# A convolution and an ELU network in one kernel: two start-up convs one step earlier, their writes ahead of the reads

## The chip, the cores and the metric

The kernel runs on one core of one Trainium2 chip. The metric is the device time of one execution in microseconds (us). A core has a tensor engine (PE in the profile; PEld is its weight load), VectorE (DVE), ScalarE (ACT), GpSimd (POOL) and SyncE (SP). Each engine works through its own list of instructions in order; engines wait for each other through semaphores. Transfers (DMA) are issued by SP (queue q1 in the profile) or by GpSimd (queue q0), and run on 16 shared DMA engines.

## What is computed

```python
# x: (8, 4096, 192), weight: (8 heads, 7 taps), w_in: (192, 2048), w_out: (2048, 192)
w = softmax(weight, axis=-1)                       # seven taps per head
x_pad = concatenate([zeros(B, 6, D), x], axis=1)   # causal
idx = arange(S)[:, None] + arange(7)[None, :]
x_unf = x_pad[:, idx, :].reshape(B, S, 7, 8, 24)
a = einsum('hk,bskhg->bshg', w, x_unf).reshape(B * S, 192)
h = a @ w_in
g = where(h > 0, h, exp(minimum(h, 0)) - 1)        # ELU
out = g @ w_out                                    # (32768, 192), float32
```

A causal convolution with seven taps per head, then a network of two layers with an ELU between, for 32768 tokens.

## The kernel before

**Super steps and steps.** The tokens are worked through in 32 super steps `s` of 1024, each in two halves `g` of 512. A super step has 16 steps, one for each 128 columns of the hidden layer; step `n` in this text counts through all of them, so that steps 0 to 15 belong to super step 0, and step 16 is the first of super step 1. One step is: PE multiplies `att` (the convolved tokens) with `w_in` in six matmuls into one of three slots of the PSUM tensor `H` (L706), ScalarE takes the exponential of both halves into `E` (L499), GpSimd limits it (L410), VectorE forms the ELU as `gT` (L561). A slot of `H` is free for step n once VectorE is through with the step that had it, three takers before. Matmuls of the second layer (L741, from `gT` and `w_out` into `ops`) for the super step before are put in the gaps between the steps, by the table `GAPS`.

**Where the convolved tokens come from.** Super step 0 makes its own with small matmuls at the start (L616 to L648). For every later super step there are two convs, one per half, numbered `m = 2*s + g - 2`: conv 0 and conv 1 are halves 0 and 1 of super step 1, conv 2 is half 0 of super step 2. A conv is 40 small matmuls on PE (L679), from a window of `x` (`xg`, loaded by GpSimd at L362 in two parts per super step) and the taps matrix `Tr`. ScalarE copies its result to `csb` (L479), and then it goes over DRAM to change its layout: SP writes `csb` into the bounce buffer in DRAM (`conv_slots`, L773, 256 KB), waits for that to have landed, and reads it back into `att` in three transfers of 64 KB (`read_att`, L334). The first step of super step 1 waits for all six reads of its two halves at L701.

**What sets the order.** The list `order` (L87 to L148) is the schedule that PE, ScalarE and SP all follow: for each step its "h" item, then the convs and second-layer pieces put there. For super step 0 the dictionary `EARLY_CONV` (L37) says after which step a conv comes: conv 0 after step 4, conv 1 after step 7, conv 2 after step 10. Convs 0 to 2 use the PSUM tensor `ops`, which is free at that time; a conv there waits for the copies of the one before (L671). ScalarE copies the first half of such a conv at its place in the order and the second half after the next step's exponentials (L488 to L503); the semaphore `s_ce` counts the second copies. In the first 13 steps PE also does pairs of warm-up matmuls on zeros ahead of a step (L694 to L696), except ahead of the two steps that follow a conv; these write into `ops` and so wait for the copies of the convs so far. Step 10 further waits for a second copy of `w_in`'s last columns (`s_wc`, L700).

**SP's loop** (L768 to L796). At a conv SP waits for its second copy (`s_ce`), issues the write, and then, for conv 0 and for every half 1, calls `read_att` at once, which waits for the write's landing (L327). For half 0 of super steps 2 and later the reads are issued at the second step of the super step before, when `att`'s other buffer is free (L782 to L784). Before the loop SP issues the tap loads and, once the last columns of `w_in` have come, the second copy of these (L766). GpSimd issues its loads at the very start in the order `w_in`, `x`, `w_out` (768 KB), the last part of `x` (L392 to L402).

Of the kernel before, what the change touches and what calls it, by code (L numbers as in the profile page):

```python
# [33 lines left out]
WARM = (9, 1)  # L34

CONV_AT = ((2, 1, 1), (10, 2, 0))
EARLY_CONV = {4: (1, 0), 7: (1, 1), 10: (2, 0)}  # L37
FREE_CONV = 3
QUAD = 4
XTW = 136  # L40
# [11 lines left out]
def bass_lightweight_conv__then__act_elu_kernel(  # L52
# [36 lines left out]
    def conv_at(s, g):  # L89
        m = 2 * s + g - 2  # L90
        if m >= FREE_CONV:
            slot_of_conv[m] = take_slot(("c", m))
        order.append(("c", m))
# [38 lines left out]
    for n in range(NP):  # L132
        s, i = divmod(n, NQ)
# [3 lines left out]
        if len(gaps) == 2:  # L137
            order.append(("o", gaps.pop(0)))
        if n in EARLY_CONV:
            conv_at(*EARLY_CONV[n])  # L140
        if s:
# [44 lines left out]
    with ExitStack() as stack:  # L186
# [111 lines left out]
        def load_first(eng, k):  # L298
            eng.dma_start(
                xf[:, k, :, :].rearrange("p i d -> p (i d)"),  # L300
                x_flat[GS * k : GS * (k + 1), :].rearrange("(p i) d -> p (i d)", i=QUAD),
            ).then_inc(s_xl[k], 16)

        def conv_read(W, m):
            W(s_ce, m + 1)

        def out_group(eng, t, half, g, kb=None):
            b = (2 * t + half) % 2
            row = SUP * t + GS * g + 2 * P * half
            if kb is not None:  # L310
                eng.dma_start(
                    out[row + P * kb : row + P * (kb + 1), :], osb[:, b, g, kb, :]
                ).then_inc(s_out[b], 16)
                return
            dst = out[row : row + 2 * P, :].rearrange("(k p) d -> p k d", p=P)
            if t == 0:
                dst = bass.AP(
                    tensor=out.tensor,
                    offset=(GS * half + 1 - g) * D,
                    ap=[[QUAD * D, P], [2 * D, 2], [1, D]],  # L320
                )
            eng.dma_start(dst, osb[:, b, g, :, :]).then_inc(s_out[b], 16)

        def read_att(eng, W, s, g):

            m = 2 * s + g - 2
            W(s_dw[m % 4], 16 * (m // 4 + 1))  # L327
            for j in range(3):
                src = bass.AP(
                    tensor=bounce.tensor,  # L330
                    offset=(2 * P * (s % 2) + j) * SUP + GS * g,
                    ap=[[SLOT * SUP, HEADS], [3 * SUP, 8], [1, GS]],
                )
                eng.dma_start(  # L334
                    att[HP * g : HP * (g + 1), s % 2, j, :], src
                ).then_inc(s_att[s % 2], 16)
# [240 lines left out]
        def _tensor(pe):  # L577
# [16 lines left out]
            def warm_pair(count):  # L594
                for _ in range(count):
                    for r in range(2):
                        pe.matmul(  # L597
                            ops[:, r, :],
                            zw[HP * r : HP * (r + 1), 0:P],
                            zw[HP * r : HP * (r + 1), :],  # L600
                            start=True,
                            stop=True,
                            tile_position=(HP * r, 0),
                        )
# [56 lines left out]
            for x_, item in enumerate(order):  # L661
# [26 lines left out]
                elif item[0] == "h":  # L688
                    n = item[1]
                    s, q = divmod(n, NQ)  # L690
                    if n == 0:
                        W(s_ha, 2)
                        W(s_hd, 2)
                    elif n < NQ + LAG and not any(n - 2 <= e < n for e in EARLY_CONV):  # L694
                        conv_read(W, sum(e < n for e in EARLY_CONV) - 1)
                        warm_pair(WARM[1])  # L696
# [55 lines left out]
        @block.sync  # L752
        def _sync(sy):
            W = Waits(sy)
            sy.dma_start(wh[:], weight[:, :]).then_inc(s_wd, 16)
            load_first(sy, 1)
            W(s_wp, 1)
            sy.dma_start(taps[:, :], zt[:, :]).then_inc(s_band, 16)
            W(s_band, 16)
            sy.dma_start(  # L760
                Tr[:, :, :],
                bass.AP(tensor=taps.tensor, offset=0, ap=[[1, P], [ZW, HEADS], [1, CW]]),
            ).then_inc(s_band, 16)
            c0, c1 = WCOLS[3]
            W(s_w[3], 16)
            sy.dma_start(w_in[HP:P, :, c0:c1], w_in[0:HP, :, c0:c1]).then_inc(s_wc, 16)  # L766

            for item in order:  # L768
                if item[0] == "c":
                    m = item[1]  # L770
                    s, g = divmod(m + 2, 2)
                    conv_read(W, m)
                    sy.dma_start(  # L773
                        bounce[s % 2, :, :, GS * g : GS * (g + 1)].rearrange("b p t -> p b t"),
                        csb[:, m % 4, :, :],
                    ).then_inc(s_dw[m % 4], 16)
                    if m == 0 or g == 1:

                        read_att(sy, W, s, g)
                elif item[0] == "h":  # L780
                    s, i = divmod(item[1], NQ)
                    if i == 1 and s >= 1 and s + 1 < NS:  # L782
                        W(s_h, NQ * s)
                        read_att(sy, W, s + 1, 0)  # L784
                elif item[0] == "o":
                    for key in item[2]:
                        t, half, kb = key
                        W(s_oev, place[key] + 1)
                        if (t, half) != (last, 1):
                            for g in range(2):  # L790
                                out_group(sy, t, half, g)
                        elif kb == 0:
                            for g in range(2):
                                out_group(sy, t, half, g, 0)
                        else:
                            out_group(sy, t, half, 0, 1)  # L796
            for b in range(2):
                sy.wait_ge(s_out[b], 32 * NS + 32 * b)
# [28 lines left out]
```

## Time and profile before

| | us |
|---|---|
| median of 5 runs | 752.3 |
| the five runs | 752.3, 750.1, 752.6, 749.66, 752.91 |
| the profiled execution, its time | 752.89 |
| the profiled execution, its span | 751.1 |
| matmuls of the first layer, L706 (3072) | 408.5 busy |
| matmuls of the second layer, L741 (8064) | 417.9 busy |
| exponentials, L499 (1024) | 546.2 busy |
| ELU on VectorE, L561 (1024) | 633.2 busy |
| granted TensorE clock, mean | 0.997 of full |

Times in the profile are in microseconds from the start of the span. A row of groups or of the timeline names the line, the engine, the operation and its tiles; matmuls overlap each other, so the sum of their busy times can be more than PE's. A row of waits says which engine at which line waited for whom: in total, how many times, the longest. The chain of waits is followed back from the last instruction: each piece is the work or the transfer that the next one waited for. In the table of busy time by stretch the last columns are the granted clock of TensorE (1.00 is full), the share of the DMA engines and what they moved in GB/s. The DMA queues are given with packets, megabytes and the time that their packets took as a share of 16 engines' span.

### The profile page before, as it was taken

Reading aid. Unit: us, or ns where it says so; the run is one execution under the profiler, and the core shown is the slowest. Engines: PE = TensorE matmul, PEld = TensorE weight load, DVE = VectorE, ACT = ScalarE, POOL = GpSimd, SP = SyncE. Lnnn points to the kernel's source line nnn. Section 1 sums busy time; section 2 is a strip of 40 time slices with the busy share of each in tenths; the row PEclk is TensorE's granted clock in tenths of the full one; section 3 lists DMA queues with packets and bytes.
Section 4 is the critical chain, followed back from the end, with each engine's and each line's share of the span. In section 5 each row is a group of like instructions: output and inputs, shape, how many; then the busy total and the mean of one; then the engine's idle time right before and its main releaser. Section 6 shows DMA issues by size and latency. Waiting matters only on the chain.

```text
span 751.1 us, 32212 instructions
## 1 busy us (share of the span) xinstructions
PE 737.5 (98%) x13850; PEld 517.9 (69%) x13850; DVE 638.2 (85%) x1041; ACT 646.9 (86%) x1165; POOL 661.3 (88%) x1107
## 2 busy tenths in 40 slices
PE   8699999999999999999999999999999999999998
PEld 4367777776777776776777776777776777777666
DVE  5779889889888898898898898898898898898894
ACT  6788888888888988888988888888888888888884
POOL 8789899899899899899898899898899898998883
PEclk9999999999999999999999999999999999999999
DMA  9544434535435535434435345445344344344112
GB/s 176 119 86 102 93 97 103 108 80 108 86 94 112 106 73 118 86 90 112 98 86 117 80 95 108 92 96 114 77 102 107 87 102 102 88 103 105 60 44 65
DMA packets 107039, 72.79 MB, mean 97 GB/s; under 512 B 44553, under 2 KB 106641, under 8 KB 106897
## 3 DMA queue, kind: packets, MB, share of 16 engines
q1 hardware_dynamic: 66384, 54.47, 23.9%
q0 software_dynamic: 40224, 15.78, 19.5%
q8 instruction: 108, 1.77, 1.0%
q10 hardware_dynamic: 288, 0.49, 0.2%
q14 instruction: 35, 0.28, 0.1%
HBM read 44.78 MB, written 41.42 MB: 115 GB/s over the span
## 4 chain that ended last, share of the span: by engine, by line
PE 96%; DMA 2%; ACT 1%; DVE 0%; SPq 0%; issue 0%; POOL 0%
PE ops L741 45%; PE H L706 45%; PE H L679 5%; DMA conv_slots<-csb 1%; PE H L741 1%; DMA xf<-in_x_dram 0%; SPq L334 0%; DMA att<-conv_slots 0%; DVE gT L561 0%; ACT E L499 0%; PE H L648 0%; PE ops L648 0%; ACT csb L479 0%; POOL E L410 0%; ACT xT L438 0%
## 5 line engine op out<-in xcount | busy, mean ns | idle before, releaser
L561 DVE SCALAR_TENSOR_TENSOR gT<-E,H 128x512 f16<-128x512 f32 x1024 | 633.2, 682 | 97.6 <-POOL E L410 91.3
L410 POOL TENSOR_SCALAR E<-E 128x512 f32<-128x512 f32 x1024 | 604.5, 614 | 77.4 <-ACT E L499 72.5
L499 ACT ACTIVATE E<-H 128x512 f32<-128x512 f32 x1024 | 546.2, 605 | 88.8 <-PE H L706 80.2
L741 PEld LDWEIGHTS ops<-w_out,gT 64*128 64x128 f16 x8064 | 346.2, 94 | 107.0 <-ACT osb L470 10.9
L741 PE MATMUL ops<-w_out,gT 64*128 64x192 f16 x8064 | 417.9, 243 | 0.3
L706 PE MATMUL H<-att,w_in 64*128 64x512 bf16 x3072 | 408.5, 377 | 6.3 <-DMA att<-conv_slots 3.6
L706 PEld LDWEIGHTS H<-att,w_in 64*128 64x128 bf16 x3072 | 133.8, 94 | 104.0 <-issue 5.3
L479 ACT ACTIVATE csb<-H 128x1024 bf16<-128x1024 f32 x59 | 60.4, 1024 | 0.0
L470 ACT ACTIVATE osb<-ops 128x768 f32<-128x768 f32 x63 | 51.5, 817 | 6.2 <-PE ops L741 6.2
L362 POOL DMA_DIRECT2D xg<-in_x_dram x62 | 52.3, 843 | 0.4 <-issue 0.4
L679 PE MATMUL H<-Tr,xg 128*24 128x122 bf16 (+1 forms) x2360 | 38.6, 209 | 0.0
L679 PEld LDWEIGHTS H<-Tr,xg 128*24 128x24 bf16 x2360 | 29.5, 92 | 9.3 <-issue 9.3
L741 PE MATMUL H<-w_out,gT 64*128 64x192 f16 x128 | 5.9, 243 | 0.0
L572 DVE COPY osb<-H 128x192 f32<-128x192 f32 x1 | 0.4, 358 | 6.3 <-PE H L741 6.3
L741 PEld LDWEIGHTS H<-w_out,gT 64*128 64x128 f16 x128 | 5.3, 94 | 0.0
L592 PE MATMUL ops<-zw 128*128 128x512 bf16 x9 | 4.0, 628 | 1.2 <-DVE zw L511 1.2
L367 POOL DMA_DIRECT2D w_in<-in_moe_w_in_dram x7 | 4.6, 658 | 0.3 <-DMA wh<-in_weight_dram 0.3
L597 PE MATMUL ops<-zw 64*128 64x512 bf16 x12 | 2.3, 379 | 1.6 <-ACT csb L479 1.6
L479 ACT ACTIVATE csb<-ops 128x512 bf16<-128x512 f32 x6 | 3.7, 622 | 0.0
L592 PEld LDWEIGHTS ops<-zw 128*128 128x128 bf16 x9 | 1.2, 139 | 3.2 <-issue 2.0
L597 PEld LDWEIGHTS ops<-zw 64*128 64x128 bf16 x12 | 0.6, 93 | 3.0 <-ACT csb L479 2.6
L679 PEld LDWEIGHTS ops<-Tr,xg 128*24 128x24 bf16 x120 | 1.5, 92 | 1.3 <-issue 1.3
(47 smaller groups left out, 25.9 us busy)
## 6 DMA issues: line engine op xcount, KB each, us to landing
out_dram<-osb SPq DMA_DIRECT2D x126, 192.0 KB, 2.7
conv_slots<-csb SPq DMA_DIRECT2D x62, 256.0 KB, 2.5
att<-conv_slots SPq DMA_DIRECT2D x186, 64.0 KB
xg<-in_x_dram POOLq DMA_DIRECT2D x31, 240.0 KB, 5.2
xg<-in_x_dram POOLq DMA_DIRECT2D x31, 192.0 KB, 4.5
w_out<-in_moe_w_out_dram POOLq DMA_DIRECT2D x1, 768.0 KB, 15.2
w_in<-in_moe_w_in_dram POOLq DMA_DIRECT2D x2, 240.0 KB, 8.0
xf<-in_x_dram ACTq DMA_DIRECT2D x1, 384.0 KB, 3.2
```

Of the source, the lines that this page charges most:

```text
L362: g.dma_start(xg[:, b, w0:w1, :], src).then_inc(s_x[b][part - 1], 16)
L367: g.dma_start(w_in[HP * r : HP * (r + 1), :, c0:c1], moe_w_in.rearrange("(p j) f -> p j f", j=3)[:, :, c0:c1],).then_inc(s_w[k], 16)
L410: g.tensor_scalar(out=E[:, n % NE, u, :], in0=E[:, n % NE, u, :], scalar1=1.0, scalar2=0.0, op0=ALU.min, op1=ALU.max,).then_inc(s_clp)
L470: a.activation(osb[:, b, :, :, :].rearrange("p g k d -> p g (k d)"), ops[:, :, 0 : 2 * D], ACT.Copy,).then_inc(s_oev)
L479: return a.activation(csb[:, m % 4, b0:b1, :], conv_bank(m)[:, b0:b1, :], ACT.Copy)
L499: a.activation(E[:, n % NE, u, :], H[:, k, GS * u : GS * (u + 1)], ACT.Exp).then_inc(s_exp)
L561: v.scalar_tensor_tensor(out=gT[:, s % NG3, q, u, :], in0=E[:, n % NE, u, :], scalar=1.0, in1=H[:, slot_of_pair[n] % 3, GS * u : GS * (u + ...
L592: pe.matmul(ops[:, 0, :], zw[:, 0:P], zw[:], start=True, stop=True)
L597: pe.matmul(ops[:, r, :], zw[HP * r : HP * (r + 1), 0:P], zw[HP * r : HP * (r + 1), :], start=True, stop=True, tile_position=(HP * r, 0),)
L679: ins = pe.matmul(to[SLOT * q : SLOT * q + CPH, hb, o : o + nc_], xg[:, s % NXB, w, CPH * h : CPH * (h + 1)], Tr[:, h, CW - c0 - nc_ : CW ...
L706: ins = pe.matmul(H[:, k % 3, GS * r : GS * (r + 1)], w_in[HP * r : HP * (r + 1), j, FC * q : FC * (q + 1)], att[HP * r : HP * (r + 1), s ...
L741: ins = pe.matmul(acc[:, g, d0 : d0 + D], gT[HP * rt : HP * (rt + 1), t % NG3, q, g, t0 : t0 + P], w_out[HP * rt : HP * (rt + 1), q, :], s ...
```

## The change

Conv 0 moves from after step 4 to after step 3, and conv 1 from after step 7 to after step 6; conv 2 stays. The pairs of warm-up matmuls follow the convs: before there is one ahead of each of steps 1, 2, 3, 4, 7 and 10, after the change ahead of 1, 2, 3, 6, 9 and 10. On SP, conv 0's write is no longer followed by its reads. At conv 1 SP issues the write of conv 1, then the three reads of conv 0's half, then the three of conv 1's half. Each group of reads still waits for the landing of its own write. All later convs are written and read as before.

```diff
 CONV_AT = ((2, 1, 1), (10, 2, 0))
-EARLY_CONV = {4: (1, 0), 7: (1, 1), 10: (2, 0)}
+EARLY_CONV = {3: (1, 0), 6: (1, 1), 10: (2, 0)}
...
                         csb[:, m % 4, :, :],
                     ).then_inc(s_dw[m % 4], 16)
-                    if m == 0 or g == 1:
-
+                    if m == 1:
+                        read_att(sy, W, s, 0)
+                    if g == 1:
                         read_att(sy, W, s, g)
```

## The prediction

> **What bounds the kernel now.** I read the page's busy shares first, then the waits, then the chain that ended last. The first line below is the page's, the two under it are from the waits of the whole run:
>
> ```profile
> PE 737.5 (98%) x13850; PEld 517.9 (69%) x13850; DVE 638.2 (85%) x1041; ACT 646.9 (86%) x1165; POOL 661.3 (88%) x1107
> ```
> ```profile
> PE H L706 <- DMA att<-conv_slots: 3.6, 1, 3.6
> PE H L706 <- DVE gT L561: 1.9, 4, 0.8
> ```
>
> TensorE (PE) is busy 98% of the span, and its one long wait is a single stall of 3.6 us at L706, for att. Between 42 and 735 us its waits come out empty, so time taken out before 42 us reaches the end whole. The stall is at step 16, the first step of the second super step. The chain of waits between 15 and 37 us says what it waits for (columns: start, length, what):
>
> ```profile
> 19.45 7.26 DMA conv_slots<-csb
> ...
> 26.73 0.67 SPq L334
> ...
> 28.70 2.72 DMA conv_slots<-csb
> ...
> 31.44 0.58 SPq L334
> ...
> 32.69 2.83 DMA att<-conv_slots
> ...
> 35.57 0.88 PE H L706 x6
> ```
>
> SP works in order. It writes conv 0 (19.45) and waits 7.26 us for it to land. It issues the three reads of half 0 (26.73 to 28.66), only then writes conv 1 (28.70), waits 2.72 us, and issues the three reads of half 1 (31.44 on). The last of these, issued at 32.69, lands 2.83 us later and step 16 starts at 35.57. Conv 1's data had been in SBUF since ScalarE finished it at 23.60 (22.96 + 0.64): its write stood 5.1 us in SP's queue behind conv 0's landing and reads.
>
> The stall has a second price, in the busy time by stretch (columns: stretch, its length, PE, PEld, DVE, ACT, POOL busy, then the granted clock):
>
> ```profile
> 18.00:20.00 2.00, 1.25 (x12) 0.40 (x12) 1.88 (x4) 2.00 (x5) 1.45 (x4) 1.00 1.61 194
> 22.00:24.00 2.00, 1.15 (x8) 0.29 (x8) 1.82 (x4) 2.00 (x6) 1.62 (x3) 1.00 1.11 290
> 36.20:36.40 0.20, 0.20 (x5) 0.16 (x3) 0.00 (x0) 0.00 (x0) 0.00 (x0) 0.52 0.00 0
> 36.40:39.60 3.20, 3.20 (x35) 2.31 (x31) 1.28 (x2) 1.96 (x4) 1.39 (x3) 0.50 0.21 61
> ```
>
> After the stall the granted clock falls to half for 3.4 us while PE is busy throughout; before it, with stalls of 0.75 and 0.85 us (19.48 and 23.66), it stays at 1.00. The loss is 0.20 x 0.48 + 3.20 x 0.50 + 0.20 x 0.05 = 1.71 us (the next 0.2 us had 0.95).
>
> **The change, part by part.**
>
> *SP's order.* Conv 1's write no longer stands behind conv 0's reads. From the first read to step 16's start it was 35.57 - 26.73 = 8.84 us, of which conv 1's turn (issue to the next read's start) took 31.44 - 28.70 = 2.74. If conv 1 has landed by the time SP comes to its reads, that turn is gone: 26.73 + 8.84 - 2.74 = 32.83. The six reads keep their issue time, 1.97 us for the first three and 1.25 up to the sixth.
>
> Has it landed? SP comes to half 1's reads at 26.73 + 1.97 = 28.70. Conv 1's write can go out when its second half is copied. I walk ScalarE and PE with the rows before: two Exp take about 1.1 us, a half copy adds 0.6. Conv 0 runs at about 14.98 instead of 16.26 (0.65 us of PE; one warm-up pair of 0.38 moves away from there to step 9). Its first half copy follows step 3's Exp (to 16.3), step 4's Exp end near 17.85, its second half at 18.45, 0.97 earlier than the 19.42 of before. Step 6's warm-up pair waits for that, conv 1 follows at about 19.4 instead of 20.44, and its second half ends near 22.8 instead of 23.60. So the write goes out at 22.8. In light traffic it took 2.72 us, which makes 25.5. Two things are in its way: conv 0's packets ahead of it, and a remnant of the weight loads. The queue's packets by stretch show conv 0's almost through by 24.25, with two stragglers at 25.6 behind the GpSimd queue's last ones. That puts conv 1 at 26.7 to 28. It is covered if it lands by 28.70; past that each microsecond costs one.
>
> *Conv 0 earlier.* Does its write land before 26.71? It is issued at about 18.55 instead of 19.45, behind the w_in copy that SP issues at 17.82 in both kernels. [...]
>
> ```profile
> q0 software_dynamic: 2022, 0.77, 160.3%
> q1 hardware_dynamic: 1, 0.00, 0.1%
> ```
>
> The w_in copy lay in SP's queue (q1) since 17.82, conv 0's write since 19.45, and one packet moved in four microseconds; both went out once q0's bulk was through at 22. [...] I take the row. It is this queue at this moment.
>
> *PE's and ScalarE's work in the start.* The same 80 conv matmuls and four half copies, moved by one step; the same six warm-up pairs (before at steps 1, 2, 3, 4, 7, 10, now 1, 2, 3, 6, 9, 10). A wait for a copy stands three steps behind its conv in both (7 and 10 before, 6 and 9 now). The cover for the moves is step 10: it waits for the w_in copy, which arrives at 24.2 in both kernels, and by my walk ScalarE comes to step 10's Exp at 24.95 against the 25.06 of before. A walk wrong by 0.1 us is hidden there, and by up to 0.8 more in what is left of the stall at step 16 (below); past both, a microsecond costs one. From step 10 on the order is the same, and PE is ready for step 16 at 35.57 - 3.56 = 32.01. The landing of the taps matrix isn't shown, only that conv 0 did not wait at 16.26: the moved conv 0 could wait at most 1.28 us, at least nothing. I take nothing, since that queue's packets are through by 13. Conv 1 needs the second x load, landed at 7.33 + 9.2 = 16.5.
>
> *Waits added.* SP now waits for conv 1's copy (22.8) ahead of conv 0's reads; behind it stand those reads, which couldn't go before 26.71 anyway: 3.9 us of cover, free. Conv 2's write, behind the reads, comes at about 30.5 instead of 33.31, so super step 2's first reads (waiting for its landing until 36.29) only get earlier. It still follows the last read at the same 0.6 us, so it disturbs that read no more than before. GpSimd's and VectorE's queues are not touched.
>
> *The sum.* Step 16 starts at 32.83 with PE ready at 32.01, so 0.82 us of stall stay: a gain of 35.57 - 32.83 = 2.74. A stall of 0.82 is like the 0.75 and 0.85 that left the clock at 1.00, and unlike the 3.56 that halved it, so the 1.71 comes back too: PE was the busy engine in that stretch, and in later super steps the same steps go through at full clock without a wait. Together 4.45 us. The profiled execution has a span of 751.1 and a time of 752.89 (1.79 lie around the span); less 4.45 they are 746.65 and 748.44. The median of the runs is 752.3, so 747.85.
>
> [...] The median lies with the profiled time, which did lose it, so I keep the 1.71.
>
> **The rivals.**
> - [...] Chance 0.17.
> - *The wait for conv 1 takes the place of the turn removed*, in part: conv 1 meets the same traffic as conv 0 did and needs its 7.26 us. It lands at 22.8 + 7.26 = 30.06, 1.36 past the cover; gain 3.1, 749.2. Another microsecond late makes it 750.2. Against: after 24.25 the queues were almost idle. Chance 0.14.
> - *The clock is not kept, or the median loses it in neither kernel*: gain 2.74, about 749.6. Chance 0.08.
> - *Slower:* the added traffic delays a landing. Conv 1's packets now share the remnant of the load with conv 0's, and half 1 can't be read until both are in. It is even at a landing of 31.44 and slower by over 0.3% (2.26 us, with the clock lost again) only from 28.70 + 5.00 = 33.7, where step 16 starts at 37.83. That is 10.9 us after its issue, against 7.26 for a write that sat through the starved stretch; price there +2.3, 754.6. Chance 0.03.
> - *It does not do what it says*: the order of SP's instructions, as built, has two writes and then six reads; conv 0's write alone could be no earlier, which is my main case already.
>
> **How the numbers follow.** Main case 0.58, at 747.85. Its run-to-run spread, seen before (749.66 to 752.91), mostly comes with this stall, so I allow 0.6 below the floor of 747.0, 746.4. Above, the range reaches over the late landing and the clock case to 750.0. Over 0.3% (2.26 us, about what a measurement of this kernel can tell from no change) faster is below 750.04: the main case, the floor, most of the late landings and of the clock case, 0.86. Within 0.3%: the rest, 0.10. Slower 0.04.
>
> **What would show it.** In the profile after: two writes at about 18.5 and 22.8 and six reads from 26.7 without a gap between the third and the fourth; step 16 at 32.8 with a stall near 0.8; the granted clock at 1.00 between 33 and 40 us; the rest of the span as before, shifted by 4.5. I am wrong if conv 0 lands elsewhere than at 26.7 (the queue's starvation is the step I can check least), if SP stands for conv 1 after the third read, or if the clock falls anyway.

## The result and the profile after

The changed kernel takes 748.24 us (median of 21 runs, 747.56 to 750.57), the kernel before 751.92 us in the 40 runs beside it (749.18 to 755.95): 0.996 of the time, 95% interval 0.995 to 0.997, or 3.7 us less at the medians. The prediction said 747.85, 4.45 less. The profiled executions differ by 4.7: span 751.1 before, 746.4 after (748.14 as a time).

The page's busy shares hardly move. PE has lost 2.4 us of busy time (737.5 before), about 1.7 of it through the stretch at half clock (worked out below):

```profile
PE 735.1 (98%) x13850; PEld 517.0 (69%) x13850; DVE 638.0 (85%) x1041; ACT 646.8 (87%) x1165; POOL 659.2 (88%) x1107
```

In the waits of the whole run the 3.6 us for att at L706 are gone. Apart from 0.6 us for ScalarE's first att tile, this line is all that PE's first-layer matmuls still wait for others:

```profile
PE H L706 <- DVE gT L561: 1.9, 4, 0.8
```

SP's timeline (start, length from the first issue to the end of the last, operation) shows the new order: two writes, of which the second went out at 23.4, six reads without a gap between third and fourth, conv 2's write.

```profile
17.57 0.72 SPq L766 DMA_DIRECT2D w_in<-w_in  x1
18.34 5.45 SPq L773 DMA_DIRECT2D conv_slots<-csb  x2
25.43 3.78 SPq L334 DMA_DIRECT2D att<-conv_slots  x6
29.25 0.45 SPq L773 DMA_DIRECT2D conv_slots<-csb  x1
```

Between 15 and 37 us the chain of waits no longer runs through a DMA. It runs through the start's own work, and has a gap of 0.90 us in PE in the middle of conv 1 that is put down to issue (time in which the profile shows nothing that PE waits for):

```profile
19.37 0.54 PE ops L679 x35
19.91 0.90 issue
20.80 0.23 PE ops L679 x4
...
22.80 0.60 ACT csb L479
...
24.62 3.74 DVE gT L561 x6
...
28.41 0.82 PE H L706 x6
...
32.67 0.65 PE H L706 x6
```

Step 16 starts at 32.51 in PE's timeline, with no stall (the chain counts it from the end of the matmuls before, 32.67):

```profile
32.51 0.81 PE L706 MATMUL H<-att,w_in 64*128 64x512 bf16 x6
```

In the busy time by stretch the clock stays up where it had halved:

```profile
33.00:40.00 7.00, 7.00 (x148) 4.97 (x146) 5.87 (x10) 6.29 (x12) 6.50 (x11) 1.00 0.26 71
```

One figure ties all these traces together: the time from step 16's start to the start of VectorE's last copy (L572), since PE has no wait of note between. VectorE's timeline, first after, then before:

```profile
742.92 0.36 DVE L572 COPY osb<-H 128x192 f32<-128x192 f32 x1 [6.27 <-PE H L741]
```
```profile
747.66 0.36 DVE L572 COPY osb<-H 128x192 f32<-128x192 f32 x1 [6.27 <-PE H L741]
```

It is 742.92 - 32.51 = 710.41 after, 747.66 - 35.57 = 712.09 before. So the 4.7 us are 35.57 - 32.51 = 3.06 of earlier start and 1.68 of clock.

### The profile page after: what moved, and what is told of

The parts are those of the page before. It is cut to its first block, busy times and chain, and to the rows that moved or that the text cites. A ratio compares the mean times of both kernels' runs of the same rounds, so it can differ in the third digit from the quotient of the medians.

```text
span 746.4 us, 32212 instructions
## 1 busy us (share of the span) xinstructions
PE 735.1 (98%) x13850; PEld 517.0 (69%) x13850; DVE 638.0 (85%) x1041; ACT 646.8 (87%) x1165; POOL 659.2 (88%) x1107
## 3 DMA queue, kind: packets, MB, share of 16 engines
q0 software_dynamic: 40224, 15.78, 19.6%
## 4 chain that ended last, share of the span: by engine, by line
PE 97%; DVE 1%; ACT 1%; DMA 1%; issue 0%; POOL 0%; SPq 0%
PE ops L741 45%; PE H L706 45%; PE H L679 5%; PE H L741 1%; DVE gT L561 1%; DMA xf<-in_x_dram 1%; ACT E L499 0%; PE H L648 0%; ACT csb L479 0%; POOL E L410 0%; PE ops L648 0%; PE ops L679 0%; ACT xT L438 0%; PE H L616 0%; DVE xh L536 0%
## 5 line engine op out<-in xcount | busy, mean ns | idle before, releaser
L706 PE MATMUL H<-att,w_in 64*128 64x512 bf16 x3072 | 407.7, 377 | 2.5 <-DVE gT L561 1.9
L706 PEld LDWEIGHTS H<-att,w_in 64*128 64x128 bf16 x3072 | 134.0, 94 | 99.3 <-issue 5.8
L679 PE MATMUL H<-Tr,xg 128*24 128x122 bf16 (+1 forms) x2360 | 38.6, 209 | 0.0
L679 PEld LDWEIGHTS H<-Tr,xg 128*24 128x24 bf16 x2360 | 29.5, 92 | 9.3 <-issue 9.3
L572 DVE COPY osb<-H 128x192 f32<-128x192 f32 x1 | 0.4, 358 | 6.3 <-PE H L741 6.3
L679 PEld LDWEIGHTS ops<-Tr,xg 128*24 128x24 bf16 x120 | 1.6, 92 | 2.3 <-issue 2.3
L679 PE MATMUL ops<-Tr,xg 128*24 128x122 bf16 (+1 forms) x120 | 2.1, 209 | 0.9 <-issue 0.9
```

The lines of the kernel that those rows point to most:

```text
L679: ins = pe.matmul(to[SLOT * q : SLOT * q + CPH, hb, o : o + nc_], xg[:, s % NXB, w, CPH * h : CPH * (h + 1)], Tr[:, h, CW - c0 - nc_ : CW ...
L706: ins = pe.matmul(H[:, k % 3, GS * r : GS * (r + 1)], w_in[HP * r : HP * (r + 1), j, FC * q : FC * (q + 1)], att[HP * r : HP * (r + 1), s ...
```

## The experiments

My theory was that SP's order is the gain, in two parts: conv 1's turn (from its write's issue to the first of its reads) leaves the chain, and a shorter stall leaves the clock up. The rivals were that the earlier convs do it, and that the clock costs nothing on the path. Each experiment was timed beside the kernel before on the same chip; ratios are against that.

**SP's order alone.** The changed kernel with

```diff
-EARLY_CONV = {3: (1, 0), 6: (1, 1), 10: (2, 0)}
+EARLY_CONV = {4: (1, 0), 7: (1, 1), 10: (2, 0)}
```

> The changed order on SP (two writes, then six reads) with conv 0 and 1 left after steps 4 and 7. My theory (conv 1's turn of 2.74 us taken out of SP's chain, and the clock kept): the second write goes out at about 23.6, step 16 starts by 32.8, the granted clock stays at 1.00, and nearly the whole gain of the change is here: 3.2 to 4 us under the kernel before. Rival (the earlier convs are what brings the att tiles in time): conv 0 lands as late as before, step 16 still stalls by more than 1.5 us, gain under 2 us.

Measured: 747.89 against 751.11, ratio 0.9960 (0.9947 to 0.9974). SP's timeline and PE's:

```profile
21.37 4.54 SPq L773 DMA_DIRECT2D conv_slots<-csb  x2
26.18 3.78 SPq L334 DMA_DIRECT2D att<-conv_slots  x6
```
```profile
12.70 0.82 PE L706 MATMUL H<-att,w_in 64*128 64x512 bf16 x6 [0.56 <-ACT att L447]
...
33.55 0.82 PE L706 MATMUL H<-att,w_in 64*128 64x512 bf16 x6
```

There is no stall at step 16, and the whole gain is here. The clock alone cannot be it: the 22 executions of the kernel before that kept their mean clock at 0.999 or more beside it have a median of 750.41, still 2.5 us more. Two things I had not foreseen. The second write goes out at 25.6, not 23.6; it has landed 2.1 us later, before SP comes to its reads. And PE's first step is at 12.70, not 10.8 (second fence): PE is still 1.6 us late at step 15, and step 16 starts at 33.55 because PE comes then.

**The earlier convs alone.** The kernel before with `EARLY_CONV` of the changed one.

> Conv 0 and 1 after steps 3 and 6, but SP keeps its old order (write, reads, write, reads). My theory: conv 0 lands between 25.4 and 26.7, conv 1's turn of 2.7 stays in the chain, step 16 starts between 34.2 and 35.5 with a stall of 2 to 3 us; gain 0 to 2 us, more only where the clock happens to be kept. Rival (the earlier issue is served earlier, and that is the gain): step 16 at 33 or before, gain 3 us or more.

Measured: 750.35 against 751.11, ratio 0.9992 (0.9984 to 1.0001): not told from no change. (More of its executions kept the clock, 18 of 22 at 0.999 or more against 22 of 46 of the kernel before beside it.) Its waits still have the stall, 2.30 us before step 16 at 34.28:

```profile
PE H L706 <- DMA att<-conv_slots: 2.3, 1, 2.3
```

Conv 0 landed at 25.37 and conv 1's turn then took 2.7, as the theory has it. The clock stayed up after this stall:

```profile
34.00:35.00 1.00, 0.72 (x8) 0.37 (x10) 0.18 (x1) 0.00 (x0) 0.00 (x0) 1.00 0.15 44
35.00:36.00 1.00, 1.00 (x20) 0.72 (x18) 0.00 (x0) 0.86 (x2) 0.18 (x1) 1.00 0.00 0
```

**The kernel before, kept warm.** Ahead of step 16's wait for att, in its own slot of `H` (the call is shortened here):

```diff
+if n == NQ:
+    wait_slot(k)
+    for _ in range(14):
+        for r in range(2):
+            pe.matmul(H[:, k % 3, GS * r : GS * (r + 1)], zw[HP * r : HP * (r + 1), 0:P], ...)
```

> The kernel before, with 14 pairs of matmuls on zeros put into step 16's own slot of H ahead of its wait for att (about 3.0 us of PE work, overwritten by step 16). The stall's end stays where it was (about 35.6), but PE is not idle. If the clock's fall is a price of the stall of its own: granted clock 1.00 throughout, and 1.7 us less than those executions of before that lost it, about 750.5. If it costs nothing on the path: same as before, 752. If the two groups in the times of before (around 749.9 and 752.2) are executions with and without the clock's fall: the times here have one group only.

Measured: 752.07 against 751.11, ratio 1.0009 (1.0001 to 1.0018): not the 1.7 us less that I expected. By the number it is the rival's outcome, but the block itself is why. PE's timeline:

```profile
32.84 3.20 PE L706 MATMUL H<-zw 64*128 64x512 bf16 x28
35.87 0.81 PE L718 MATMUL H<-att,w_in 64*128 64x512 bf16 x6
```

In this execution PE started late (first step at 12.08). The last read was issued at about 31.7, and between 35 and 36 us the DMA engines moved nothing (share 0.30 between 34 and 35, then 0.00). PE went straight from the block into step 16 at 35.87: the block had taken the stall's place and overran it. The clock stayed: in 21 of 22 executions it was 0.999 or 1.000, and from step 16 to the last copy it took 746.22 - 35.87 = 710.35. The median can't price the clock here.

**The same with a short block**, 6 pairs instead of 14.

> The kernel before with only 6 pairs on zeros (1.3 us) ahead of step 16's wait, so that they end before the att tiles land even where PE comes late to step 16; PE's idle stretch shrinks from 3.56 to about 2.3 us. If the clock's fall is a price of its own, paid in those executions of before that show a granted clock of 0.998 or less: no execution shows 0.997 any more, the times form one group at 749.5 to 751.2, median about 750.4, and step 16 to the end of the span takes 713.8 us as in the changed kernel, not 715.5 as in the profile of before. If the clock costs nothing on the path: two groups as before.

Measured: 751.28 against 750.84, ratio 1.0007 (0.9995 to 1.0020): again no gain, and 7 of 14 executions had a clock of 0.997 or 0.998. Two more executions of this kernel and two of the kernel before were traced to say why.

> The kernel before with 6 pairs on zeros ahead of step 16's wait, a second look. In the five-round run 5 of its 14 executions took 752.7 to 753.6 with a clock of 0.997 or 0.998, which I had not expected. If it falls among these: either the clock fell at the start (5 to 12 us), or it fell after step 16 although PE's idle stretch was under 2.3 us, or the reads landed a microsecond or two later; the trace tells which.

The first took 752.93. Its chain and its clock:

```profile
32.83 2.75 DMA att<-conv_slots
35.63 1.32 PE H L718 x6
36.95 0.96 PE ops L753 x12
37.91 1.28 PE H L718 x6
39.19 0.91 PE ops L753 x20
```
```profile
36.40:39.40 3.00, 3.00 (x30) 1.82 (x28) 1.09 (x2) 1.26 (x3) 1.19 (x2) 0.53 0.20 59
```

It is the second of the causes that I had listed: the clock fell after an idle stretch of only 2.27 us, behind 1.47 us of matmuls on zeros. The earlier convs alone had 2.30 us idle at the same place and kept it. From step 16 to the last copy it took 747.71 - 35.63 = 712.08 here.

> As the look before it: 750 to 751.5 with the clock kept, or 752.7 to 753.6 with one of the three causes named there.

The second took 750.89: idle 1.40, clock kept, 745.66 - 35.26 = 710.40.

**The kernel before, traced twice more.**

> The kernel before again, one look, to see a second execution of it in a trace. Executions of before come out near 750.4 with a granted clock of 0.999 or 1.000 and near 752.3 with 0.997 or 0.998. My theory now: PE's start differs (the first step at 10.8 or at 12 to 12.7 us, by whether its clock is up at the small matmuls of the start), the chain of DMAs ends at about 35 in both. With the early start the stall at step 16 is over 3 us and the clock falls after it: 752 or more. With the late start the stall is 1.5 to 2.5 us, the clock stays and the time is 750 to 751. Step 16 to VectorE's last copy: 710.4 us where the clock stays, 712.1 where it falls.

It took 750.5, with a late start (first step at 12.76). Its chain:

```profile
21.43 4.40 DMA conv_slots<-csb
...
27.80 2.50 DMA conv_slots<-csb
...
34.85 0.82 PE H L706 x6
```

The stall was 1.19 (I had expected 1.5 to 2.5), the clock was kept after it, and 745.25 - 34.85 = 710.40. Its mean clock of 0.998 comes from the start, in the busy time by stretch:

```profile
5.00:10.00 5.00, 3.60 (x58) 3.07 (x60) 1.78 (x3) 1.56 (x4) 5.00 (x8) 0.77 1.10 142
10.00:15.00 5.00, 4.43 (x52) 2.88 (x50) 1.16 (x3) 2.08 (x5) 2.52 (x4) 0.89 1.30 189
```

> As the look before it: either early start, stall over 3 us, clock falls, 752 or more; or late start, stall 1.5 to 2.5 us, clock kept, 750 to 751.

It took 749.59, and is neither of my two cases: early start (10.88), but conv 0 landed at 25.66, so step 16 began at 33.92 after a stall of only 1.48:

```profile
19.55 6.11 DMA conv_slots<-csb
...
33.92 0.82 PE H L706 x6
```

**The changed kernel on the chip of the first three experiments.**

> The changed kernel itself, beside the other three on one chip. 747.6 to 748.7, with an occasional execution 1 to 2 us longer. Its profile again has no stall at step 16 and the clock at 1.00; whether PE's gap of 0.90 us in the middle of conv 1, put down to issue, and conv 0's landing 7.1 us after its issue come again is open.

748.33 against 751.11, ratio 0.9961 (0.9947 to 0.9976). There is no stall and the clock is up. PE's gap of 0.90 in conv 1 did not come again, but PE's start is late (12.14), and step 16 is at 32.88.

**What holds conv 0's write.** The kernel before, with w_out's load cut to the first of its 16 row blocks. VectorE sets the others to zero, so that most of the second layer is left out of the result:

```diff
-w_out[:, :, :], moe_w_out.rearrange("(q p) d -> p q d", p=FC)
+w_out[:, 0:1, :], moe_w_out[0:FC, :].rearrange("(q p) d -> p q d", p=FC)
...
+v.memset(w_out[:, 1:NQ, :], 0.0)
```

> The kernel before with its old SP order, but GpSimd loads only the first of the 16 row blocks of w_out (the other 15 are set to zero by VectorE: that part of the second layer is left out of the result). It tests what holds conv 0's write. If the GpSimd queue's bulk starves SP's queue: the w_in copy and conv 0's write go through at once, conv 0 lands 2.5 to 3 us after its issue (near 22.5, not 25.4 to 26.7), the whole chain of writes and reads moves up by 3 to 4 us, and step 16 has at most a short stall even in the old order; time about 748. If conv 0's landing has another cause: it still takes 5 us or more, and the time stays at 750 or above.

Measured: 747.65 against 750.84, ratio 0.9957 (0.9944 to 0.9971), the whole gain of the change, in SP's old order. SP's timeline, and the queues between 18 and 22 us:

```profile
21.06 0.38 SPq L774 DMA_DIRECT2D conv_slots<-csb  x1
23.24 1.93 SPq L334 DMA_DIRECT2D att<-conv_slots  x3
25.24 0.43 SPq L774 DMA_DIRECT2D conv_slots<-csb  x1
27.74 1.83 SPq L334 DMA_DIRECT2D att<-conv_slots  x3
```
```profile
q1 hardware_dynamic: 218, 0.31, 34.1%
q0 software_dynamic: 303, 0.11, 23.3%
```

Conv 0's write lands 2.2 us after its issue, and conv 1's turn (25.24 to 27.74), still there in SP's order, no longer matters: step 16 has no stall.

**Is the start the new limit?** SP's order alone (convs after steps 4 and 7), without the pairs on zeros ahead of steps 7 and 10:

```diff
-elif n < NQ + LAG and not any(n - 2 <= e < n for e in EARLY_CONV):
+elif n < 5:
```

> The changed SP order with convs at steps 4 and 7, and without the pairs on zeros at steps 7 and 10, which make PE wait for ScalarE's copies. After the change the end of the wait at step 16 is set by the start itself (PE comes to it at 32 to 33.5, the tiles land before). If PE's waits of 0.75 and 0.85 us for the copies hold that up: 0.3 to 0.9 us less than the SP order alone, about 747.3. Rival (ScalarE and VectorE are the pace of the start, PE's waits are covered): the same 747.9.

748.17 against 750.84, ratio 0.9966 (0.9955 to 0.9977): nothing gained over 0.9960. Its chain shows what covers PE's waits for the copies, the w_in copy ahead of step 10:

```profile
18.21 6.36 DMA w_in<-w_in
24.57 0.05 issue
24.61 0.84 PE H L706 x6
```

Last, one more warm-up matmul at the very start (`WARM = (10, 1)` in the changed kernel):

> The changed kernel with ten instead of nine warm-up matmuls at the very start (the nine end at 4.7 to 5.2, PE then idles to 5.6 to 6.0 for the first x tile). After the change step 16 starts when PE comes to it, so a start at 10.8 instead of 12 to 12.7 us should reach the end. If the short idle stretch at 5.2 us is what lets the clock stay or fall low in about half of the executions: fewer late starts, median 0.3 to 0.8 us under the changed kernel's 748.2 to 748.3, no execution with a granted clock of 0.998. If not: the same 748.2 to 748.5.

748.10 against 750.61, ratio 0.9961 (0.9949 to 0.9974). The six executions all had a clock of 0.999 or 1.000, but 7 of 7 and 19 of 21 of the changed kernel had too: not told from it. Its trace has an early start (10.81), and step 16 comes earlier than in any other:

```profile
31.98 0.81 PE L706 MATMUL H<-att,w_in 64*128 64x512 bf16 x6
```

## Why the prediction was right, and where it was off

**SP's order (right).** Conv 1's turn left the chain, its landing was covered, and this alone is the gain. The earlier convs add nothing that the runs can tell.

**Conv 1's write (right, later than walked).** 22.8 was forecast. It went out at 23.4 in the profile, 0.6 later, behind PE's gap of 0.90 in conv 1, which no trace of before shows. It landed 3.0 us later, at 26.4, and SP came to its reads only at 27.3.

**Conv 0's landing (wrong, by 1.28 us).** The forecast kept the landing of before, 26.71, for a write expected 0.9 us earlier, because of the row of the queues of before: between 18 and 22 us SP's moved 1 packet and GpSimd's 2022. It landed at 25.43. Landings in the traces with the earlier convs and all of w_out: 25.43, 25.37, 25.39, 24.91, for issues at 18.3 to 19.6. With convs at steps 4 and 7: 26.71, 25.83, 25.66, 26.18, 25.93, 26.71, 27.04, 25.59 and 26.26, for issues at 19.5 to 21.4. So the single trace that I built on lay late in a spread of 1.5 us, and the means of the two groups differ by about 1 us. And yet SP's queue starved after the change too, between 18 and 22 us:

```profile
q0 software_dynamic: 1926, 0.73, 154.0%
q1 hardware_dynamic: 29, 0.04, 3.5%
q8 instruction: 1, 0.02, 1.5%
```

With most of w_out's load gone SP's queue moved 218 packets in the same stretch: the load is the cause of the starvation. The time of issue alone does not set the landing: with convs at steps 4 and 7, writes issued at 20.3 to 21.4 landed at 25.8 to 26.3, those issued at 19.5 to 19.8 at 25.6 to 27.0. Why the earlier convs' writes land about 1 us earlier is not settled.

**Step 16's start (32.83 forecast, 32.51 seen) by two errors that cancel.** The forecast left 0.82 us of stall. Conv 0's landing 1.28 earlier took the DMA chain off the end; PE came 0.50 later than the 32.01 that I took from before. That the two errors together leave only 0.32 us is luck. The chain now ends in the start's own work, and the 0.50 goes with the gap in conv 1: with one more warm-up matmul PE has 0.4 of such idle time at L679 in its place, and PE came at 31.98; the twelve other traces have none. What makes the gap is open: the profile after has one packet of the instruction queue (q8) between 18 and 19 us, while the kernel before, the first three experiments and the changed kernel on their chip have none between 18 and 22. So the stall went entirely, to which I had given a chance of 0.17 with step 16 at 32.01; PE came later than that. The range's floor of 747.0 stands for this case, the median of 752.3 less 3.56 of stall and 1.71 of clock; no run of the changed kernel shows it, the fastest took 747.55.

**The clock (right in the profile, mis-sized in the median).** 1.71 was forecast, 1.68 seen between the two profiles. What was off is "the median lies with the profiled time, which did lose it, so I keep the 1.71". Of 72 executions of before on two chips, 35 have a clock of 0.999 or more with a median of 750.46, and 37 one of 0.998 or less with 752.05 (some of these may have lost it at the start instead, as the traced execution of 750.5 did). Medians of before came out at 751.92, 751.11, 750.84 and 750.61. So the profile of before was a dear execution: late landing, early PE, 3.56 us of stall and the clock lost, 4.7 us over the profile after. At the medians the gain is 3.7 us where it was first measured (21 runs after) and 2.8 on the chip of the first experiments (7 runs). Neither of my two kernels with matmuls on zeros turned the clock into a gain at the median: that part of the cause is shown by the traces (712.09 and 712.08 with the fall; 710.3 to 710.6 in the twelve other traces), not by an experiment that forces it.

## What to carry to other kernels

When a queue works in order, look for transfers that are ready but stand behind another's landing: putting the second write ahead of the first one's reads costs nothing, because here the reads could not go yet anyway (the second write went out at 23.4, the first landed at 25.4). Before a median is forecast from one profile, ask which of its terms vary: a stall that ends on a DMA and a clock that falls after it are two such terms, and the profile may hold both at their worst. Once a stall is gone, the next limit decides what more the same repair can bring; here it was the start, and moving the convs brought nothing on top that the runs can tell.

## What the hardware showed that I had not expected

- The clock fell after an idle stretch of 2.27 us (behind matmuls on zeros) and stayed after one of 2.30 at the same place; it fell after 3.56. The length of the stretch alone does not tell these apart; what does is open. At the start the granted clock was 0.78 and 0.77 between 5 and 10 us in two traces, with slow matmuls from 7.67 and 7.79 us on; PE's longest wait since its warm-up matmuls was 0.96 and 1.12 us there, while waits of 1.07 and 1.2 us left two others at 1.00. PE's timeline of the traced execution of 750.5:

```profile
6.07 0.53 PE L616 MATMUL H<-ident,xh 128*64 128x2 bf16 x9 [1.12 <-DVE xh L536]
7.79 1.89 PE L648 MATMUL ops<-xT,Dg 64*128 64x256 bf16 x16 [0.33 <-ACT xT L438]
```

- PE's first step began at 10.8 to 11.1 us in eight traces and at 11.7 to 12.8 in six, up to 2.0 us apart. In five of the six the small matmuls of the start were slower (sixteen of L648 took 1.7 to 1.9 us and not 1.06); in the sixth, at 11.65, the first tile of x came later (VectorE waited 1.9 us for it, 1.3 to 1.8 in the others). In two of the five the granted clock was 0.77 or 0.78 between 5 and 10 us; in the other three the profile has it at 1.00, and what slowed them is open. In the kernel before, the wait for att swallows most of this (1.19 us of stall with the start at 12.76, 3.56 with 10.78); in the changed kernel it reaches step 16 (32.51 with the early start and the gap, 32.88 with the late start).
- With the whole of w_out, in the profiles of both kernels, the first three experiments and the changed kernel on their chip, SP's queue moved 1 to 29 packets between 18 and 22 us while GpSimd's queue moved 1926 to 2022, although the w_in copy had been issued into SP's queue by 18.07 at the latest. Without most of w_out it was 218 to 303.
